# Weights loaded from their fourth byte on and rebuilt by a shift and a half-precision copy, keys transposed in the MLP's PSUM ring, another order of the steps

## The chip, the cores and the metric

The kernel runs on one core of one Trainium2 chip. The metric is the device time of one execution in microseconds (us), as a median of several runs. The engines of the core are named as in the profile: PE (TensorE matmul), PEld (TensorE weight load, which overlaps PE), DVE (VectorE), ACT (ScalarE), POOL (GpSimd) and SP (SyncE, which issues the transfers).

## What is computed

A gated linear attention (a recurrence over 768 tokens for 4 batches of 8 heads of width 48) is followed by a two-layer MLP with an unusual activation. Cut to what matters:

```python
for t in range(S):                                     # S = 768
    state = alpha[:, :, t, :, None] * state + einsum('bhd,bhe->bhde', k[:, :, t], v[:, :, t])
    y[:, :, t] = einsum('bhd,bhde->bhe', q[:, :, t], state)
x = y.transpose(0, 2, 1, 3).reshape(3072, 384)
h = x @ w_in                                           # 384 x 2048, float64 in memory
sp = maximum(h, 0) + log1p(exp(-abs(h)))
out = (h * erf(sp)) @ w_out                            # 2048 x 384, float64 in memory
```

The two weight matrices arrive as float64, everything else as float32.

## The kernel before

**Attention.** The tokens are cut into 24 chunks (`Chunk`, number n). A chunk loads alpha, k, q and v (`la lk lq lv`), makes decay products with two scans on DVE (`sb`, `sa`), scales k and q (`kk`, `qq`), and then on PE transposes the keys (`pn`, copied out by `kn` on ACT or `kd` on DVE), multiplies the state into the output (`qt`), makes scores (`ps`, masked on DVE by `mk`), multiplies scores by values (`sv`) and makes the state's update (`pu`, added on DVE by `ta` to the state that `td` has decayed). `pn`, `ps` and `pu` all write one PSUM tile, `both`. The output is copied to SBUF in two parts that together hold float32: `xh` on ACT (x_hi) and `xl` on DVE (x_lo, the remainder). `xp` and `xe` are another way to x_lo: PE subtracts x_hi in PSUM, ACT copies the rest out.

**MLP.** Two chunks make one of 12 blocks (`Moe`, 256 tokens). In a block each of 8 halves of the hidden units takes `hm` on PE (18 matmuls of 128x256 into a PSUM ring `h` of two buffers), `he` on ACT or `hd` on DVE (copy to SBUF), then by pairs of halves the activation: `u n1 n2 n3 g` on ACT, which switch between two function tables, and `ma mb z1 z2` on DVE. After that comes `ga` on ACT or `gd` on DVE (high part), `gl` on DVE (low part), and `om` on PE (12 matmuls of 128x384, added up in the two PSUM tiles `acc0` and `acc1`). `oe` on ACT or `ob` on DVE copies the sums out, `od` stores them. There is one pair of accumulators, so the first `om` of a block waits for the copies of the block before.

**Weights.** 12 tiles of w_in (512 columns) and 16 of w_out (384 columns) are made once (`Weight`, steps `w..i_n` and `w..o_n`). `wl` loads float64 as pairs of 32-bit words. ACT makes a float32 from the high word (`wy`) and the three bits of the low word (`wc`, or `wv` on DVE); DVE joins them (`wa`, `wb`); ACT rounds to the matmul's type (`wh`, or `wk` on DVE). The remainder is made on DVE (`wq`) or by two matmuls on PE into the ring `h` (`wp`) and a copy (`we`). The first `hm` of a group of hidden units needs its three tiles of w_in complete.

**Order.** All of it is one list of step names, `ORDER`, written out by hand or by a planner. Each engine runs its instructions in the order of the list (class `Queue`), so an instruction that waits holds everything behind it on its engine. `dw_n` are n matmuls on the identity that write nothing used.

Of the kernel before, what the change touches and what calls it, by code (L numbers as in the profile page):

```python
# [16 lines left out]
I16 = mybir.dt.int16  # L17
# [38 lines left out]
hm_2_0_1 who_13 wqo_13 z2_0_3 wco_14 ma_1_0 pn_6 he_2_0_1 wyo_14 wlo_15 wco_15 wyo_15 wao_14 om_0_2_1 kn_6 sv_6
ga_0_3_0 gl_0_3_0 pu_6 wao_15 ga_0_3_1 gl_0_3_1 xh_6 wbo_14 lv_7 om_0_3_0 u_1_1 lk_7 wbo_15 g_1_0 mb_1_0
hm_2_2_0 ic_6 la_7 who_15 wqo_15 who_14 wqo_14 om_0_3_1 u_1_2 n1_1_2 oe_0_1 od_0_1 oe_0_0 hm_2_2_1 z1_1_0 z2_1_0
ga_1_0_0 sb_7 lq_7 rc_7 gl_1_0_0 gd_1_0_1 n1_1_1 lq_8 xl_6 sa_7 gl_1_0_1 om_1_0_0 n2_1_2 n2_1_1 om_1_0_1
he_2_2_0 qq_7 kk_7 hm_2_3_0 n3_1_1 td_7 ma_1_1 mb_1_1 n3_1_2 he_2_2_1 ps_7 mk_7 qt_7 hm_2_3_1 g_1_1 u_1_3 z1_1_1  # L60
z2_1_1 u_2_1 ic_7 ga_1_1_0 sv_7 xh_7 ta_6 la_8 ga_1_1_1 lv_8 ma_1_2 pn_7 gl_1_1_0 om_1_1_0 gl_1_1_1 om_1_1_1
sb_8 he_2_3_0 mb_1_2 g_1_2 n1_1_3 he_2_3_1 n2_1_3 n3_1_3 lk_8 xl_7 hm_3_0_0 hm_3_0_1 z1_1_2 z2_1_2 rc_8 gd_1_2_0
gl_1_2_0 om_1_2_0 ma_1_3 he_3_0_0 ga_1_2_1 gl_1_2_1 om_1_2_1 g_1_3 he_3_0_1 td_8 hm_3_1_0 hm_3_1_1 mb_1_3 sa_8
u_2_0 n1_2_0 lk_9 n2_2_0 z1_1_3 z2_1_3 gd_1_3_1 kk_8 ga_1_3_0 la_9 gl_1_3_0 om_1_3_0 n3_2_0 lq_9 qq_8 kn_7
n1_2_1 n2_2_1 n3_2_1 he_3_1_0 od_0_0 he_3_1_1 gl_1_3_1 pu_7 ps_8 ma_2_0 qt_8 mb_2_0 om_1_3_1 sb_9 ma_2_1 mb_2_1
g_2_1 z1_2_1 ob_1_0 od_1_0 u_2_2 oe_1_1 hm_3_2_0 mk_8 z2_2_1 hm_3_2_1 g_2_0 ic_8 rc_9 gd_2_1_1 u_2_3 n1_2_2 sv_8
gd_2_1_0 gl_2_1_1 gl_2_1_0 xh_8 n2_2_2 ta_7 om_2_1_0 pn_8 z1_2_0 he_3_2_0 ic_9 sa_9 om_2_1_1 he_3_2_1 z2_2_0
gd_2_0_1 gl_2_0_1 n3_2_2 n1_2_3 kk_9 xl_8 lv_9 ma_2_2 hm_3_3_0 hm_3_3_1 ga_2_0_0 n2_2_3 n3_2_3 kn_8 qq_9 g_2_2
om_2_0_1 mb_2_2 td_9 qt_9 pu_8 ps_9 ma_2_3 gl_2_0_0 om_2_0_0 u_3_1 u_3_0 z1_2_2 he_3_3_1 mk_9 sv_9 g_2_3
he_3_3_0 lq_10 n1_3_0 z2_2_2 gd_2_2_0 gl_2_2_0 om_2_2_0 od_1_1 la_10 mb_2_3 gd_2_2_1 xh_9 sb_10 xl_9 hm_4_0_0  # L70
rc_10 n1_3_1 n2_3_1 n2_3_0 gl_2_2_1 n3_3_0 n3_3_1 sa_10 he_4_0_0 ta_8 ma_3_0 hm_4_0_1 he_4_0_1 om_2_2_1 g_3_0
z1_2_3 z2_2_3 ga_2_3_0 mb_3_0 u_3_2 ga_2_3_1 z1_3_0 hm_4_2_0 hm_4_2_1 ma_3_1 lk_10 kk_10 u_3_3 qq_10 he_4_2_0
la_11 gl_2_3_0 g_3_1 n1_3_3 pn_9 kn_9 gl_2_3_1 n2_3_3 n3_3_3 om_2_3_0 td_10 om_2_3_1 oe_2_1 oe_2_0 qt_10 lk_11
z2_3_0 mb_3_1 z1_3_1 hd_4_2_1 z2_3_1 gd_3_1_0 sb_11 gl_3_1_0 ga_3_0_1 pu_9 ps_10 mk_10 ta_9 gl_3_0_1 n1_3_2
n2_3_2 n3_3_2 ic_10 rc_11 ic_11 hm_4_1_0 he_4_1_0 lv_11 hm_4_1_1 td_11 he_4_1_1 om_3_1_0 ma_3_2 pn_10 ga_3_0_0
gl_3_0_0 u_4_0 om_3_0_1 od_2_1 g_3_2 sa_11 u_4_1 mb_3_2 z1_3_2 ga_3_1_1 ma_3_3 g_3_3 lq_12 gl_3_1_1 z2_3_2
hm_4_3_0 hm_4_3_1 om_3_1_1 om_3_0_0 u_4_2 n1_4_2 ga_3_2_1 kd_10 lv_10 pu_10 n1_4_1 n2_4_1 kk_11 la_12 mb_3_3
lq_11 qq_11 ps_11 sv_10 xh_10 sb_12 he_4_3_1 gl_3_2_1 om_3_2_1 gd_3_2_0 gl_3_2_0 mk_11 ta_10 rc_12 xl_10 z1_3_3
z2_3_3 gd_3_3_1 od_2_0 pn_11 n1_4_0 n2_4_0 om_3_2_0 kn_11 gl_3_3_1 n3_4_0 ga_3_3_0 gl_3_3_0 qt_11 ma_4_0 pu_11
# [12 lines left out]
lq_15 sb_15 om_5_1_1 rc_15 gl_5_2_0 ma_5_3 u_6_2 pn_14 u_6_1 td_15 om_5_2_0 gd_5_0_0 kn_14 sv_14 sa_15 qq_15
# [51 lines left out]
def gla_moe(ctx: ExitStack, tc: tile.TileContext, q, k, v, alpha, w_in, w_out, out):  # L144
    nc = tc.nc


    M, CPB, P, NP, NI, TC = q.shape
    B, H, S = M * NI, 2 * NP, CPB * TC
    W = NP * NI * TC  # L150
    NT, DM = out.shape
    FF = w_in.shape[1]
    TB = 256
    NBLK = NT // TB
    KT = DM // P
    NF = FF // P
    GT = 4
    NG = NF // GT
# [485 lines left out]
    class Weight:  # L644
# [23 lines left out]
        def wx(self):  # L668
            self.wy(on_dve)
# [277 lines left out]
```

## Time and profile before

| | us |
|---|---|
| median of 3 runs (lowest, highest) | 516.27 (515.26, 516.82) |
| span of the profiled execution, first to last instruction | 513.9 |
| PE busy in the span | 504.0 (98%) |
| PEld busy | 481.7 (94%) |
| DVE busy | 488.2 (95%) |
| ACT busy | 465.8 (91%), of it 64 table loads: 82.1 |

The profiled execution has no time beside its span; the median of the runs is 2.35 us above that span, which is taken for what lies around it. "Busy" is the share of the span in which an engine had an instruction running. Matmuls are pipelined, so a busy PE is not a PE at its peak; the time that PE needs is read from the distance between the starts of groups of matmuls. An instruction that starts before the one ahead of it has ended overlaps it: sums of durations are larger than busy time.

### The profile page before, as it was taken

The page shows a single profiled execution, that of the slowest core. Times are in us where ns is not written, and L with a number is a line of the kernel's source. Part 1 is how long each engine was busy: PE and PEld are TensorE (multiplying, and loading weights), DVE is VectorE, ACT ScalarE, POOL GpSimd, SP SyncE. Part 2 cuts the span into 40 slices and gives each one's busy share as a digit, 9 for nine tenths or more (in the row PEclk, how much of TensorE's full clock was granted, in tenths as well). Part 3 has the DMA queues.
Part 4 walks back from the last instruction along what each step waited for, and adds up shares of the span by engine and source line. Part 5 has one row for each costly group of instructions (what it writes and reads, how often), then busy time and mean ns, then how long its engine had stood idle before and what let it go on. Part 6 is the DMA issues. An engine that isn't in the chain of part 4 may idle for free.

```text
span 513.9 us, 16869 instructions
## 1 busy us (share of the span) xinstructions
PE 504.0 (98%) x7465; PEld 481.7 (94%) x7465; DVE 488.2 (95%) x655; ACT 465.8 (91%) x637; POOL 6.5 (1%) x41
## 2 busy tenths in 40 slices
PE   6999999999999999999999999999999999999996
PEld 6689999999999999999999999999999999999996
DVE  6999999999999999999999999999998999999894
ACT  6999999999999989999898888899988899898992
POOL 3000000000000000000000000000000000000000
PEclk9999999999999999999999999999999999999999
DMA  8954363321121032122023211301231310000000
GB/s 324 401 200 176 117 188 131 97 81 60 58 74 44 22 99 78 45 73 83 23 78 107 80 41 60 85 15 44 68 111 54 90 58 32 3 1 32 0 32 34
DMA packets 21387, 43.69 MB, mean 85 GB/s; under 512 B 2368, under 2 KB 5440, under 8 KB 21312
## 3 DMA queue, kind: packets, MB, share of 16 engines
q1 hardware_dynamic: 21312, 42.59, 25.4%
q8 instruction: 59, 0.97, 0.8%
q14 instruction: 16, 0.13, 0.1%
HBM read 37.86 MB, written 4.72 MB: 83 GB/s over the span
## 4 chain that ended last, share of the span: by engine, by line
PE 64%; DVE 18%; ACT 12%; issue 4%; DMA 1%; POOL 1%; DVEq 0%; POOLq 0%; ACTq 0%
PE acc L211 29%; PE h__112 L211 13%; PE h__111 L211 12%; PE both L211 4%; PE py L211 4%; DVE t L211 2%; DVE gl__104 L211 1%; ACT L211 1%; DVE gl__103 L211 1%; DVE w__98 L211 1%; DVE w__100 L211 1%; PE warm L211 1%; ACT w__97 L211 1%; DMA s__87<-in_moe_w_out_dram 1%; DVE w__97 L211 1%
## 5 line engine op out<-in xcount | busy, mean ns | idle before, releaser
L211 ACT ACT_TABLE_LOAD x64 | 82.1, 1283 | 1.9 <-PEq L901 0.9
L211 PE MATMUL acc<-wo_hi,gh__102 128*128 128x384 f32 x192 | 44.7, 346 | 0.1
L211 PE MATMUL acc<-wo_hi,gh__101 128*128 128x384 f32 x192 | 43.9, 348 | 0.1
L211 PE MATMUL acc<-wo_lo,gh__102 128*128 128x384 f32 x192 | 43.0, 337 | 0.2 <-DVE wo_lo L211 0.2
L211 PE MATMUL acc<-wo_hi,gl__104 128*128 128x384 f32 x192 | 43.1, 337 | 0.0
L211 PE MATMUL acc<-wo_lo,gh__101 128*128 128x384 f32 x192 | 41.6, 336 | 0.0
L211 PE MATMUL acc<-wo_hi,gl__103 128*128 128x384 f32 x192 | 41.6, 337 | 0.0
L211 PEld LDWEIGHTS acc<-wo_lo,gh__102 128*128 128x128 f32 x192 | 34.2, 188 | 0.5 <-DVE wo_lo L211 0.5
L211 PEld LDWEIGHTS acc<-wo_hi,gl__104 128*128 128x128 f32 x192 | 34.3, 188 | 0.0
L211 PEld LDWEIGHTS acc<-wo_hi,gl__103 128*128 128x128 f32 x192 | 34.0, 188 | 0.2 <-DVE gl__103 L211 0.2
L211 PEld LDWEIGHTS acc<-wo_lo,gh__101 128*128 128x128 f32 x192 | 34.1, 188 | 0.0
L211 PEld LDWEIGHTS acc<-wo_hi,gh__101 128*128 128x128 f32 x192 | 31.6, 188 | 1.9 <-DVE gh__101 L211 0.4
L211 PEld LDWEIGHTS acc<-wo_hi,gh__102 128*128 128x128 f32 x192 | 32.6, 188 | 0.8 <-DVE gh__102 L211 0.2
L211 DVE TENSOR_TENSOR_SCAN B<-raw_a,back 128x520 f32<-128x520 f32 x24 | 29.6, 1233 | 4.0 <-POOL T L266 3.9
L211 DVE TENSOR_TENSOR_SCAN A<-raw_a,start 128x520 f32<-128x520 f32 x24 | 29.6, 1233 | 0.2
L211 ACT ACTIVATE s__88<-s__88 128x1024 f32<-128x1024 f32 x22 | 23.2, 1056 | 1.0 <-DVE t L211 0.9
L211 ACT ACTIVATE s__86<-s__86 128x1024 f32<-128x1024 f32 x20 | 21.2, 1058 | 1.9 <-DVE t L211 1.8
L211 PE MATMUL h__112<-x_hi__107,wi_hi 128*128 128x256 f32 x144 | 21.7, 286 | 0.3 <-ACT wi_lo L211 0.3
L211 PE MATMUL h__111<-x_hi__107,wi_hi 128*128 128x256 f32 x144 | 21.4, 284 | 0.0
L211 PE MATMUL h__111<-x_hi__108,wi_hi 128*128 128x256 f32 x144 | 21.1, 282 | 0.0
L211 PE MATMUL h__112<-x_hi__108,wi_hi 128*128 128x256 f32 x144 | 21.1, 282 | 0.0
L211 PE MATMUL h__112<-x_lo__109,wi_hi 128*128 128x256 f32 x144 | 21.0, 281 | 0.0
(338 smaller groups left out, 1420.5 us busy)
## 6 DMA issues: line engine op xcount, KB each, us to landing
raw_a<-in_alpha_dram SPq DMA_DIRECT2D x24, 260.5 KB, 2.8
raw_k<-in_k_dram SPq DMA_DIRECT2D x24, 256.0 KB, 3.1
raw_q<-in_q_dram SPq DMA_DIRECT2D x24, 256.0 KB, 3.3
raw_v__113<-in_v_dram SPq DMA_DIRECT2D x12, 256.0 KB, 3.3
raw_v__114<-in_v_dram SPq DMA_DIRECT2D x12, 256.0 KB, 3.6
out_dram<-o__106 SPq DMA_DIRECT2D x12, 192.0 KB, 2.0
out_dram<-o__105 SPq DMA_DIRECT2D x12, 192.0 KB, 2.6
s__85<-in_moe_w_out_dram SPq DMA_DIRECT2D x4, 384.0 KB, 3.7
```

What stands on the lines that cost most here:

```text
L211: ins = made(*args, **kw)
```

## The change

- A weight tile is loaded from the fourth byte on, as bytes (the arrays are padded by one column for it). The first 32-bit word of a pair then holds the low 27 bits of the float32 to be made (after a shift by 5), the second its sign and high exponent in its low byte.
- `wy`, `wc`, `wv`, `wb` go. `wr` on DVE shifts the second word up into a tile of its own, `wd` on ACT copies that, as half precision, into the upper half of its own words, and `wa` on DVE shifts the first word and joins.
- Of the 28 remainders, 6 of w_in (9 before) and 3 of w_out (none before) are made on PE; three chunks use `xp` and `xe` in place of `xl`.
- `pn` writes a buffer of the MLP's PSUM ring `h` in place of `both`; the state has one tile in place of two; the ring of high parts has 4 buffers in place of 2; the hs tile is taken at `he` and no longer at `hm`.
- `dw` grows from 25 matmuls to 41, of which 30 stand first; the matmuls that clear `both` come behind the first 30.
- `ORDER` is another list. New steps that it does not use are left out below.

```diff
-    gp = Ring(gpool, gh=([P, 2, TB], F32R, 2), gl=([P, 2, TB], F32R, 2), ...
+    gp = Ring(gpool, gh=([P, 2, TB], F32R, 4), gl=([P, 2, TB], F32R, 2), ...
...
-    Ts = [[at.tile([P, NI * NP * HD], F32, name="T", tag=f"T{m}{n}", bufs=1) for n in range(2)] for m in range(M)]
+    Ts = [at.tile([P, NI * NP * HD], F32, name="T", tag=f"T{m}", bufs=1) for m in range(M)]
...
         def pn(self):
-            self.pn_ = both
+            self.pn_ = ps_h.tile([P, 512], F32, name="pn", tag="h")
...
         def hm(self, g, half):
-            if half == 0:
-                self.hs[g] = self.pl.h.tile([P, GT * TB], F32, name="hs", tag="hs")
...
         def he(self, g, half, copy=on_act):
+            if self.hs[g] is None:
+                self.hs[g] = self.pl.h.tile([P, GT * TB], F32, name="hs", tag="hs")
...
     class Weight:
+            if self.wide:
+                self.src = src.bitcast(U8)[:, 8 * c * n + 3 : 8 * (c + 1) * n + 3]
...
         def wl(self):
             if self.wide:
-                self.st = self.pool.tile([P, self.n, 2], I32, name="wst", tag=self.tag)
-                sp.dma_start(out=self.st.rearrange("p n two -> p (n two)"), in_=self.src.bitcast(I32))
+                st = self.pool.tile([P, self.n, 2], I32, name="wst", tag=self.tag)
+                flat = st.rearrange("p n two -> p (n two)").bitcast(U8)
+                sp.dma_start(out=flat, in_=self.src)
+                self.low, self.rest = st[:, :, 0], st[:, :, 1]
...
-        def wy(self, copy=on_act):
-            if self.wide:
-                copy(self.parts()[0], self.st[:, :, 1].bitcast(F32), 2.0**-112)
...
-        def wc(self):
-                act.activation(self.parts()[1], low[:, :, 3], AF.Copy, scale=1 / 32, bias=-31 / 64)
...
+        def wr(self):
+            if self.wide:
+                buf = keep_w.tile([P, 2, 512], F32, name="wbuf", tag="w")
+                self.top, self.z = buf[:, 0, : self.n], buf[:, 1, : self.n]
+                dve.tensor_scalar(
+                    out=self.top.bitcast(I32), in0=self.rest, scalar1=24, scalar2=None, op0=ALU.logical_shift_left
+                )
...
         def wd(self):
             if self.wide:
+                high = self.top.bitcast(F16).rearrange("p (n two) -> p n two", two=2)[:, :, 1]
+                act.activation(high, self.top, AF.Copy)
...
         def wa(self):
             if self.wide:
-                y, z = self.parts()
                 dve.scalar_tensor_tensor(
-                    out=z, in0=y.bitcast(I32), scalar=3, in1=z, op0=ALU.logical_shift_left, op1=ALU.bitwise_or
+                    out=self.z.bitcast(I32), in0=self.low, scalar=5, in1=self.top.bitcast(I32),
+                    op0=ALU.logical_shift_right, op1=ALU.bitwise_or,
                 )
...
-        def wb(self):
...
         def dw(self, n):
             for _ in range(n):
                 pe.matmul(out=self.t[:, :P], lhsT=ident, rhs=ident, start=True, stop=True)
+            for bank in range(2 * clear):
+                pe.matmul(
+                    out=both[:, bank, NP * TC : NP * (TC + D)], lhsT=ident, rhs=Ts[0][:, : NP * D],
+                    start=True, stop=True,
+                )
```

The start of DVE's instructions. In the rows w__97 to w__100 are the buffers in which weights are put together, hs__90 and up and s__85 and up are loaded weights, B and A the scans' results, sT the masked scores. Before:

```order
L211 SCALAR_TENSOR_TENSOR B<-raw_a,back 128x520
L211 RECIPROCAL start<-B 128x8
L211 SCALAR_TENSOR_TENSOR A<-raw_a,start 128x520
L211 SCALAR_TENSOR_TENSOR w__97<-w__97 128x512 x2
L211 SCALAR_TENSOR_TENSOR w__98<-w__98 128x512 x2
L211 TENSOR_TENSOR raw_k_118<-raw_k_118,B 128x512
L211 SCALAR_TENSOR_TENSOR w__99<-w__99 128x512 x2
```

The same place after the change:

```order
L203 TENSOR_SCALAR w__97<-hs__90 128x512
L203 SCALAR_TENSOR_TENSOR B<-raw_a,back 128x520
L203 RECIPROCAL start<-B 128x8
L203 SCALAR_TENSOR_TENSOR A<-raw_a,start 128x520
L203 TENSOR_SCALAR w__98<-s__85 128x384
L203 TENSOR_SCALAR w__99<-hs__91 128x512
L203 SCALAR_TENSOR_TENSOR w__97<-hs__90,w__97 128x512
L203 TENSOR_TENSOR raw_k_120<-raw_k_120,B 128x512
```

DVE now begins with a weight's shift and reads two tiles of w_in and one of w_out before the keys are scaled.

PE's instructions around the first `hm` (the row with x_hi and wi_hi) before, with `wp` (w__97 and wi_hi,minus), `pn` (ident,raw_k) and `wp` ahead of it:

```order
L211 MATMUL h__112<-w__97,ident 128x512
L211 MATMUL h__112<-wi_hi,minus 128x512
L211 MATMUL both<-ident,raw_k_119 128x128 x4
L211 MATMUL h__111<-w__100,ident 128x512
L211 MATMUL h__111<-wi_hi,minus 128x512
L211 MATMUL h__112<-x_hi__107,wi_hi 128x256 x6
```

The same place after the change:

```order
L203 MATMUL both<-raw_v__116,kn 48x48 x16
L203 MATMUL both<-raw_q_118,raw_k_120 64x64 x16
L203 MATMUL py<-raw_q_118,T 32x64 x32
L203 MATMUL h__113<-ident,raw_k_120 128x128 x4
L203 MATMUL h__114<-w__99,ident 128x512
L203 MATMUL h__114<-wi_hi,minus 128x512
L203 MATMUL h__113<-x_hi__109,wi_hi 128x256 x6
```

Chunk 2's `ps`, `qt` and `pn` and chunk 1's `pu` have moved ahead of the first `hm`; `pn` now writes `h`; the last `wp` ahead of the first `hm` is that of w_in tile 9, of the last group.

PE's instructions where block 10 ends and block 11 begins, after the change (the row with `good` is a one-column matmul of a range check):

```order
L203 MATMUL acc<-wo_hi,gh__104 128x384 x2
L203 MATMUL acc<-wo_lo,gh__104 128x384 x2
L203 MATMUL acc<-wo_hi,gl__106 128x384 x2
L203 MATMUL both<-ones,good 1x1
L203 MATMUL acc<-wo_hi,gh__101 128x384 x4
```

The last `om` of block 10 and the first of block 11 now stand side by side; before, two `hm` stood between them.

## Rows read from the trace of the kernel before

**Rows 1.** Windows: us, then busy us (instructions) of PE, PEld, DVE, ACT, POOL; PEclk, DMA share, GB/s
```profile
0.00:28.88 28.88, 23.87 (x312) 17.00 (x312) 24.39 (x39) 24.48 (x50) 4.38 (x19) 1.00 0.96 366
28.88:108.88 80.00, 79.73 (x1487) 76.07 (x1488) 79.65 (x126) 79.71 (x136) 0.49 (x5) 1.00 0.40 131
108.88:509.84 400.96, 400.41 (x5669) 388.59 (x5668) 384.21 (x492) 361.13 (x452) 1.67 (x17) 1.00 0.18 56
509.84:513.90 4.06, 0.00 (x1) 0.00 (x0) 0.00 (x0) 0.49 (x1) 0.00 (x0) 1.00 0.28 101
```

**Rows 2.** Chain that ended last: start us, us, what
```profile
9.94 1.10 PE h__111 L211 x3
...
173.50 2.08 PE acc L211 x12
175.59 2.13 PE h__112 L211 x18
...
184.64 0.79 PE py L211 x53
185.43 0.98 PE both L211 x64
186.41 2.32 PE h__112 L211 x18
```

**Rows 3.** Timeline of PE at its first MLP matmul: start us, us, what, idle before
```profile
28.88 0.99 PE L211 MATMUL h__112<-x_hi__107,wi_hi 128*128 128x256 f32 x6 [0.26 <-ACT wi_lo L211]
```

**Rows 4.** Groups by form: mean ns of the operations that weights are made of
```profile
L211 DVE SCALAR_TENSOR_TENSOR w__100<-w__100 128x384 int32<-128x384 int32 x10 | 5.5, 549 | 0.0
L211 DVE SCALAR_TENSOR_TENSOR w__97<-w__97 128x512 int32<-128x512 int32 x6 | 4.1, 681 | 0.0
L211 DVE TENSOR_SCALAR w__98<-s__85 128x384 int32<-128x384 int32 x2 | 0.7, 350 | 0.0
L211 DVE CAST gh__101<-hs__90 128x512 fp32r<-128x512 f32 x4 | 1.7, 420 | 0.1
L211 ACT ACTIVATE w__98<-hs__95 128x512 f32<-128x512 f32 x1 | 0.7, 691 | 0.0
L211 ACT ACTIVATE w__97<-s__87 128x384 f32<-128x384 f32 x2 | 1.1, 573 | 0.0
L211 ACT ACT_TABLE_LOAD x64 | 82.1, 1283 | 1.9 <-PEq L901 0.9
```

**Rows 5.** Timeline of the first microseconds: start us, us, what, idle before
```profile
0.91 0.38 SPq L211 DMA_DIRECT2D raw_a<-in_alpha_dram  x1
1.34 0.42 SPq L211 DMA_DIRECT2D hs__90<-in_moe_w_in_dram  x1
1.52 0.29 POOL masks.py:199 TENSOR_SCALAR_AFFINE_SELECT ident<-ident 128x128 f32<-128x128 f32 x1
...
3.92 1.24 DVE L211 TENSOR_TENSOR_SCAN B<-raw_a,back 128x520 f32<-128x520 f32 x1 [3.92 <-POOL T L266]
5.04 1.22 ACT L211 ACTIVATE w__97<-hs__90 128x512 f32<-128x512 f32 x2 [2.56 <-DMA hs__90<-in_moe_w_in_dram]
```

**Rows 6.** Windows of the first `dw` alone: us, busy us of PE (matmul passes), PEclk, DMA share, GB/s
```profile
4.72:8.77 4.05, 4.05 (x19) 1.00 1.03 396
8.77:9.78 1.01, 1.01 (x10) 1.00 1.01 378
```

**Rows 7.** DMA issues: KB each, median us to landing
```profile
raw_a<-in_alpha_dram SPq DMA_DIRECT2D x24, 260.5 KB, 2.8
raw_k<-in_k_dram SPq DMA_DIRECT2D x24, 256.0 KB, 3.1
```

**Rows 8.** Groups: copies out of the PSUM ring, and an activation on the same engine
```profile
L211 ACT ACTIVATE hs__90<-h__111 128x512 f32<-128x512 f32 x9 | 5.3, 585 | 0.0
L211 ACT ACTIVATE s__88<-s__88 128x1024 f32<-128x1024 f32 x22 | 23.2, 1056 | 1.0 <-DVE t L211 0.9
```

**Rows 9.** Timeline: the copy of the first accumulator at the end
```profile
508.84 0.49 ACT L211 ACTIVATE o__105<-acc 128x384 f32<-128x384 f32 x1 [3.27 <-PE acc L211]
```

More of the change, by code (lines that the diff above doesn't have):

```diff
@@ L151, in gla_moe @@
     NT, DM = out.shape
-    FF = w_in.shape[1]
+    FF = w_in.shape[1] - 1
     TB = 256
@@ L218, in __getattr__ @@
             return call
[L220 to L221 removed]
+    queues = [Queue(e) for e in (nc.tensor, nc.vector, nc.scalar, nc.sync, nc.gpsimd)]
+    pe, dve, act, sp, pool = queues
     ra = raw.tile([P, 1 + L], F32, name="raw_a")
@@ L262, in need @@
             act.preload_act_table_set(name)
-    Ts = [[at.tile([P, NI * NP * HD], F32, name="T", tag=f"T{m}{n}", bufs=1) for n in range(2)] for m in range(M)]
-    for t in Ts[0] + Ts[1]:
+    Ts = [at.tile([P, NI * NP * HD], F32, name="T", tag=f"T{m}", bufs=1) for m in range(M)]
+    for t in Ts:
         nc.gpsimd.memset(t, 0.0)
-    Tv = [[t.rearrange("p (i a d) -> p i a d", i=NI, a=NP)[:, :, :, :D] for t in pair] for pair in Ts]
+    Tv = [t.rearrange("p (i a d) -> p i a d", i=NI, a=NP)[:, :, :, :D] for t in Ts]
     both = ps_at.tile([P, 2, 512], F32, name="both", tag="b")
-    pe.matmul(
-        out=both[:, 1, NP * TC : NP * (TC + D)], lhsT=ident, rhs=Ts[0][0][:, : NP * D],
-        start=True, stop=True,
-    )
     def on_act(out, in_, scale=1.0):
@@ L450, in ta @@
             if self.first:
-                act.activation(Tv[self.m][0], U, AF.Copy)
+                act.activation(Tv[self.m], U, AF.Copy)
             else:
-                dve.tensor_tensor(out=Tv[self.m][0], in0=Tv[self.m][1], in1=U, op=ALU.add)
+                dve.tensor_tensor(out=Tv[self.m], in0=Tv[self.m], in1=U, op=ALU.add)
         def xh(self):
@@ L594, in z2, with to_hi, gh, ga @@
             )
-        def ga(self, g, half):
+        def to_hi(self, g, half, copy):
             gg = self.hs[g][:, half * 512 : (half + 1) * 512]
             gh = self.pl.gp.tile([P, 2, TB], F32R, name="gh", tag="gh")
-            act.activation(gh.rearrange("p a t -> p (a t)"), gg, AF.Copy)
+            copy(gh.rearrange("p a t -> p (a t)"), gg)
             self.gg[g, half] = gg, gh
+        def gh(self, g, half):
+            self.to_hi(g, half, lambda out, in_: pool.dma_start(out=out, in_=in_))
+        def ga(self, g, half):
+            self.to_hi(g, half, on_act)
         def gd(self, g, half):
-            gg = self.hs[g][:, half * 512 : (half + 1) * 512]
-            gh = self.pl.gp.tile([P, 2, TB], F32R, name="gh", tag="gh")
-            dve.tensor_copy(out=gh.rearrange("p a t -> p (a t)"), in_=gg)
-            self.gg[g, half] = gg, gh
+            self.to_hi(g, half, on_dve)
         def gl(self, g, half):
@@ L675, in wv @@
                 )
-        def wc(self):
-            if self.wide:
-                low = self.st.rearrange("p n two -> p (n two)").bitcast(U8).rearrange("p (n b) -> p n b", b=8)
-                act.activation(self.parts()[1], low[:, :, 3], AF.Copy, scale=1 / 32, bias=-31 / 64)
-        def halves(self, kind, k):
-            return self.parts()[1].bitcast(kind).rearrange("p (n two) -> p n two", two=2)[:, :, k]
         def wd(self):
             if self.wide:
-                act.activation(self.halves(F16, 1), self.st[:, :, 1].bitcast(F32), AF.Copy, scale=2.0**-60)
@@ L712, in wk, with wm @@
             self.wh(on_dve)
+        def wm(self):
+            pool.dma_start(out=self.hi, in_=self.z)
         def wq(self):
@@ L931 @@
                 a = wide
-        elif name == "moe_w_in":
-            a = a[order]
+        else:
+            a = _np.pad(a[order] if name == "moe_w_in" else a, ((0, 0), (0, 1)))
         a = _np.ascontiguousarray(a)
```

256 lines of the change are left out of this document (116 added, 140 removed).

## The prediction, made blind

> **What bounds the kernel now.** I read the windows first, cut at two starts: PE's first MLP matmul, and the end of its last. In [rows 1] the reader is to see three stretches. Until 28.88 us, where the first `hm` starts [rows 3], PE is busy 23.87 us, but much of that is `dw` and waiting; DVE is busy 24.39 us of the 24.96 from its first instruction at 3.92 [rows 5], and ACT 24.48. From 28.88 to 108.88 PE, DVE and ACT are all busy over 79.6 of 80 us. From 108.88 to 509.84 PE stays at 400.41 of 400.96, while DVE has 16.75 us to spare and ACT 39.8. So the time is: the front until 28.88, then 480.96 us of PE without a gap, then a tail of 4.06.
>
> Whether PE is itself the bound in the middle, or is held by DVE, the chain of waits tells: an `om` of 12 matmuls takes 2.08 us and an `hm` of 18 takes 2.13, and only one behind small matmuls takes 2.32 [rows 2]. Such rows repeat over all 96 `hm` and 96 `om`. If I give each group of matmuls behind 28.88 the median of groups of its kind with the same kinds before and behind, the 480.96 become 478.3: 2.7 us is what PE lost there to others. A change that only frees ACT or DVE cannot win more than that behind the front.
>
> **Part by part, the engines' load.** For 12 tiles of 512 and 16 of 384 columns: DVE loses `wb`, 12 x 0.681 + 16 x 0.549 = 17.0 us, and three `wv`, 1.1; it gains `wr`, a single-source shift from the same 8-byte step as `wv`: 16 x 0.350, and for 512 columns the 0.420 of a single-source copy, 5.0 [rows 4]; 10.6 together. Other steps that went to DVE (4 `kd`, 4 `hd`, 3 `wq` of w_in, and one each of `gd`, `ob`, `wk`, less 3 `wq` of w_out and 3 `xl`) add about 5. Net -2.5 of 488. ACT loses `wy` and 25 `wc` of 28, about 32.8 us at 0.69 and 0.56 to 0.57 each, and gains 28 `wd`. No row has a write of half precision with a step; the nearest are `wy`'s own 0.691 and 0.573 [rows 4], which I take: 17 us. Twice that is the upper bound; below those rows nothing on ACT speaks for a gain. But the new order switches tables 74 times for 64, 10 x 1.283 = 12.8 us [rows 4]. With 5 us of steps that went to DVE, ACT is at -8 of 466. Neither is the bound behind 108.88, so the place where this can count is the front.
>
> **The front.** Until the first `hm` DVE had 38 instructions and part of one more, which by durations are 27.1 us and took 24.39, a factor of 0.90 (instructions overlap) [rows 1]. In the new order the first `hm` needs `wq` of tile 0, and up to it stand 44: 9 + 3 `wr`, 8 + 3 `wa`, 3 each of `sb`, `rc`, `sa`, `kk`, `qq`, `mk`, 2 `wq`, 1 `td`, by durations 27.9, at 0.90 25.1 us. The load is no smaller, because three tiles of w_out and all of chunk 2's preparation now come ahead. DVE also starts later: its first instruction is now a shift of a loaded tile. That tile's load came at 5.04 when issued at 1.34 [rows 5]; issued at 0.91, 4.6. With the 0.6 us that DVE lost in this stretch before, it is through at 4.6 + 25.1 + 0.6 = 30.3. PE's last `wp` ahead of it waits for `wa` and `wh` of tile 9, some 1.7 us earlier on DVE, and takes 1.10 [rows 2], which leads to the same place. **First `hm`: 30.4**, bounds 29.2 (DVE without a pause) and 32 (below).
>
> ACT has 23.6 us of durations ahead of that point instead of 29.2, so it waits for DVE and no longer shares the bound. That is why freeing it gives nothing here. The `dw` of 30: PE starts it when POOL has made the identity, 1.85 us, and not at 3.92. Its passes take 213 ns (19 in 4.05 us, the level of 1.2 GHz) until 8.77 and then 112 ns (2.4 GHz) [rows 6], though the granted column reads 1.00 in both. If the rise comes as long after PE's first instruction as before, 4.85 us, 60 passes end at 10.8 and the four that clear `both` at 11.5. `ps` of chunk 0 waits behind them; its inputs are ready at 10.2 and DVE wants the result for `mk` at 11.95, gets it at 12.2. That 0.3 is inside the 0.6. If the rise stays at 8.77, it is 1 us more: part of the upper bound.
>
> **What PE has left.** Ahead of the first `hm` PE has now also done `ps`, `qt`, `pn` of chunk 2 and `pu` of chunk 1: 0.98 for `ps` and `pu`, 0.79 for `qt` [rows 2], and four passes of 0.112 [rows 6] for `pn`, 2.2 us. Behind it stand 480.96 - 2.2 = 478.7. Of the three `xp` one is behind it: two matmuls of 192 columns, under the 0.12 us each that 256 columns take in [rows 2] (2.13 / 18), so 0.2. Switches between large and small groups fall by a tenth in number, but fewer pass through `pn`, the only small group that costs an `hm` nothing before it: the same median count gives +0.3, bounds -1 and +1. At block 10 to 11 the accumulators must be copied with no `hm` between: DVE's copy of `acc1` (0.55 for 384 columns, as in [rows 4]) ends 0.2 to 0.5 behind the point at which PE is ready; I take 0.3. Reuse of the ring `h`, with `pn` in it: +0.3 (rival below). The state in one tile makes `ta` wait for `qt`, but `qt` stands ahead of `ta` everywhere. Together 30.4 + 478.7 + 0.2 + 0.3 + 0.3 + 0.3 = 510.2.
>
> **The tail.** Before, the copy of `acc0` ran while PE still worked on `acc1`, from 508.84 on [rows 9], and only one copy was left [rows 1]. Now ACT's list has the copy of `acc1` first, so that of `acc0`, complete a microsecond earlier, stands behind it, and its store last: +0.4. Span 510.2 + 4.06 + 0.4 = **514.7**, 0.8 above 513.9; with the median's 2.35 around it 517.0. I keep some of the 2.7 us for PE, since with 8 us less on ACT some waits will go: -0.4. **516.6.**
>
> **The loads.** Rows of 4096 and 3072 bytes now begin three bytes past a word. The transfers are near their limit in the front, 396 GB/s at a share of 1.03 [rows 6] and 0.96 over the whole of it [rows 1]. The nearest row is alpha: its rows of 2084 bytes begin at multiples of 4 that are no larger power of two, and land in 2.8 us against 3.1 for 2048 [rows 7]. I take nothing, with twice the time as the other bound.
>
> The Trainium skill speaks against the change here: "DMA: Bandwidth & Descriptors", section "How a descriptor splits into AXI transactions", says that reads start at 256-byte boundaries, so a start between them costs a transaction more. By that, an estimate, 17 in place of 16 for 4096 bytes would add 6% to each load, some 0.9 us over the 11 loads of the front if loads came last there, and the sum would be 517.5. The row of alpha shows no such cost, but its 2084 bytes were loaded alone.
>
> **Rivals.** (1) *Faster: DVE holds PE in the middle.* All three engines are full from 28.88 to 108.88. Up to the last weight step DVE's queue is 115.8 us by durations for 93.0 of PE's work, 114.5 for 88.6 before: 4.4 - 1.2 = 3.2 us in the change's favour, less 0.7 of later start. If that is what PE waits for, it gains 2.5 and most of the tail's and ring's loss is not noticed: 513.8. For it: DVE is never idle there. Against: the even 2.08 and 2.13. Chance 0.27.
> (2) *Slower: the ring `h`.* It has two buffers, and 22 `pn` are added to 105 uses. Places where PE comes back to a buffer with less than 2.2 us of its own work between: 8 before behind 25 us, all at 2.13; now 15, six of them under 2, the shortest 1.14 (block 5). A copy takes 0.585, and an activation of 1.056 ahead of it on ACT [rows 8] makes that 1.64. It decides if the copies come late by an activation in most of these places: 15 x 0.25 = 3.7 us, 520.4. Chance 0.19.
> (3) *Slower: loads from an odd byte take twice as long.* A load of 512 KB at 400 GB/s takes 1.3 us, 8 to 11 of them in the front, which has no room: 10 us or more, 527. Chance 0.08.
> (4) *The two-byte write of `wd` is slow.* At twice 17 us ACT is at +9 in all, and in the front at 29, as before; no change of the time, inside the forecast.
>
> **How the numbers follow.** Forecast 516.6 (a run of this kernel tells 0.3%, 1.55 us, from no change): chance 0.46, range 514.8 to 518.4 from the bounds of the first `hm` and of the switches. Faster by over 0.3%: rival 1, 0.27. Slower: rivals 2 and 3 and the forecast's upper end, 0.27. The range that leaves out 2 in 10 goes from 512.6 (rival 1 with 1.2 us of an early first `hm`) to 520.6.
>
> **What would show it.** The first `hm` at 30.4 (29.2 to 32), with DVE full and ACT idle some 5 us before it; `hm` and `om` at 2.13 and 2.08 behind it; the wait of `om` at block 11 under 0.5; the last two copies one behind the other. Wrong: an idle PE in front of `hm` with a copy of `h` as releaser (2), DVE waiting for transfers before 28 us (3), or PE's stretch behind the first `hm` shorter than 477 (1).

## The result and the profile after

The changed kernel takes 520.09 us in the median of 15 runs (516.85 to 523.23), the kernel before, run beside it, 515.82 (515.26 to 516.82): a ratio of 1.0078, 95% interval 1.0059 to 1.0098. It is 0.8% slower, and its runs scatter over 6.4 us where those of before scatter over 1.6. The profiled execution took 518.62 us, its span is 516.8.

The windows of the changed kernel, cut as in [rows 1] at the first `hm` and at the end of PE's last matmul (same columns):

```profile
0.00:34.22 34.22, 29.74 (x481) 23.60 (x482) 25.55 (x46) 22.38 (x46) 3.73 (x18) 1.00 0.96 353
34.22:114.22 80.00, 80.00 (x1498) 76.95 (x1497) 79.18 (x128) 79.11 (x124) 0.59 (x5) 1.00 0.44 135
114.22:511.50 397.28, 397.25 (x5529) 386.36 (x5527) 376.42 (x488) 360.00 (x444) 1.91 (x16) 1.00 0.17 51
511.50:516.80 5.30, 0.00 (x0) 0.00 (x0) 0.00 (x0) 0.87 (x2) 0.00 (x0) 0.92 0.22 77
```

Beside [rows 1]: the front is 5.34 us longer (34.22 for 28.88), PE's stretch behind it 3.68 shorter (477.28 for 480.96), the tail 1.24 longer (5.30 for 4.06). Together 2.9 us, the difference of the spans. In the longer front DVE is busy 1.2 us more and ACT 2.1 less than before; the rest of the added time those two stand idle. PE is busy 5.9 us more there, with the longer `dw` and the groups that moved ahead of `hm`.

PE's timeline in the front (start us, us, what, idle before) has two holes whose releaser is "issue", which means that PE waited for nothing that the profile shows:

```profile
18.84 0.58 PE L203 MATMUL both<-raw_v__115,kn 64*48 64x48 f32 x32
19.23 0.35 PE L203 MATMUL both<-raw_q,raw_k 48*64 48x64 f32 x9
20.58 0.57 PE L203 MATMUL both<-raw_q,raw_k 48*64 48x64 f32 x23 [0.99 <-issue]
...
29.57 0.66 PE L203 MATMUL both<-raw_q,raw_k 48*64 48x64 f32 x32
30.16 0.86 PE L203 MATMUL py<-raw_q,T 48*32 48x64 f32 x64
32.64 0.66 PE L203 MATMUL h__113<-ident,raw_k 128*128 128x128 f32 x4 [1.61 <-issue]
33.13 1.02 PE L203 MATMUL h__114<-w__99,ident 128*128 128x512 f32 x2
33.59 0.80 PE L203 MATMUL h__114<-wi_hi,minus 128*128 128x512 f32 x1
34.22 0.87 PE L203 MATMUL h__113<-x_hi__109,wi_hi 128*128 128x256 f32 x6
```

The first hole is inside one group: 9 of `ps`'s 32 matmuls run, then nothing for a microsecond, then 23. No buffer and no operand changes between the 9th and the 10th. If PE's instructions are counted from its start (weight loads, matmuls, and its sequencer's few, 7 and 13 by then), the holes stand behind the 449th and behind the 961st, 512 apart. The transfers of the stretches just ahead of the two holes (18.0 to 19.4 us, and 30.0 to 31.2) contain one packet each of another kind; columns are packets, MB, share of 16 engines:

```profile
q8 instruction: 1, 0.02, 4.6%
...
q8 instruction: 1, 0.02, 5.6%
```

By the trace's list of packets these have 16,384 bytes, which for 256 instructions is 64 bytes each, and end at 19.18 and 31.17 us. PE goes on 1.40 and 1.47 us later. The queue is PE's: it carries 60 such packets in the execution, room for 15,360 instructions, and the windows above count some 15,000 weight loads and matmuls. So the reading is that PE had run out of program. `pu` of chunk 1 with `ps` and `qt` of chunk 2 (64, 64 and 128 instructions, and two of the sequencer among them) fill the 256 up to the 961st, and PE ran through them in 1.6 us (29.18 to 30.81).

DVE's timeline in the front shows what else was late:

```profile
4.68 0.43 DVE L203 TENSOR_SCALAR w__97<-hs__90 128x512 int32<-128x512 int32 x1 [4.68 <-DMA hs__90<-in_moe_w_in_dram]
...
8.86 0.36 DVE L203 TENSOR_SCALAR w__98<-s__85 128x384 int32<-128x384 int32 x1 [0.69 <-DMA s__85<-in_moe_w_out_dram]
...
21.21 0.69 DVE L203 TENSOR_TENSOR sT<-both,mask 128x512 f32<-128x512 f32 x1 [0.81 <-PE both L203]
...
31.24 0.69 DVE L203 TENSOR_TENSOR wi_lo<-w__98,wi_hi 128x512 fp32r<-128x512 f32 x1
```

The 0.81 us at 21.21 is `mk` waiting for the `ps` that the first hole cut in two. DVE's last step for the first `hm` ends at 31.93, so DVE was not what `hm` waited for. Behind the second hole PE itself still had `pn` and `wp` to do, 1.58 us up to 34.22. Without that hole's 1.61 us `hm` would have started at 32.6, without both holes at 31.6.

At the end both copies and both stores come one behind the other (ACT and SP):

```profile
511.53 0.49 ACT L203 ACTIVATE o__108<-acc 128x384 f32<-128x384 f32 x1 [7.94 <-PE acc L203]
511.92 0.48 ACT L203 ACTIVATE o__107<-acc 128x384 f32<-128x384 f32 x1
...
512.05 0.34 SPq L203 DMA_DIRECT2D out_dram<-o__108  x1
512.48 0.38 SPq L203 DMA_DIRECT2D out_dram<-o__107  x1
```

From the last store's issue to the end of the span it is 4.3 us; before, where the two stores were issued 1.04 us apart, 3.5.

### The profile page after: what moved, and what is told of

It reads as the page before. It is cut to its first block, busy times and chain, and to the rows that moved or that the text cites. A ratio compares the mean times of both kernels' runs of the same rounds, so it can differ in the third digit from the quotient of the medians.

```text
span 516.8 us, 16909 instructions
## 1 busy us (share of the span) xinstructions
PE 507.0 (98%) x7505; PEld 486.9 (94%) x7505; DVE 481.2 (93%) x660; ACT 462.4 (89%) x614; POOL 6.2 (1%) x39
## 4 chain that ended last, share of the span: by engine, by line
PE 98%; issue 1%; ACT 0%; POOL 0%; POOLq 0%
PE acc L203 39%; PE h__113 L203 23%; PE h__114 L203 22%; PE py L203 7%; PE both L203 5%; PE warm L203 2%; ACT o__108 L203 0%; ACT o__107 L203 0%; POOL ident masks.py:199 0%; POOL inv L235 0%; POOL mask L221 0%; POOL ident masks.py:197 0%; POOL sums L233 0%; POOLq L919 0%; POOL ones L230 0%
## 5 line engine op out<-in xcount | busy, mean ns | idle before, releaser
L203 PE MATMUL acc<-wo_hi,gl__106 128*128 128x384 f32 x192 | 43.1, 337 | 0.0
L203 PE MATMUL acc<-wo_hi,gl__105 128*128 128x384 f32 x192 | 41.5, 337 | 0.0
L203 PEld LDWEIGHTS acc<-wo_hi,gl__106 128*128 128x128 f32 x192 | 34.2, 188 | 0.0
L203 PEld LDWEIGHTS acc<-wo_hi,gl__105 128*128 128x128 f32 x192 | 34.0, 188 | 0.1
L203 PE MATMUL h__113<-x_hi__109,wi_hi 128*128 128x256 f32 x162 | 24.4, 286 | 0.0
L203 PE MATMUL h__113<-x_hi__109,wi_lo 128*128 128x256 f32 x162 | 23.6, 281 | 0.0
L203 PE MATMUL h__113<-x_lo__111,wi_hi 128*128 128x256 f32 x162 | 23.5, 280 | 0.0
L203 PE MATMUL acc<-wo_hi,gh__104 128*128 128x384 f32 x96 | 22.7, 339 | 0.0
L203 PE MATMUL acc<-wo_lo,gh__104 128*128 128x384 f32 x96 | 22.4, 337 | 0.0
L203 PE MATMUL h__114<-x_hi__110,wi_hi 128*128 128x256 f32 x150 | 22.4, 285 | 0.0
L203 PEld LDWEIGHTS h__113<-x_hi__109,wi_hi 128*128 128x128 f32 x162 | 21.7, 188 | 0.7 <-ACT kn L203 0.2
L203 PE MATMUL h__114<-x_hi__110,wi_lo 128*128 128x256 f32 x150 | 21.8, 281 | 0.0
L203 PE MATMUL h__114<-x_lo__112,wi_hi 128*128 128x256 f32 x150 | 21.8, 281 | 0.0
L203 ACT ACTIVATE s__88<-s__88 128x1024 f32<-128x1024 f32 x20 | 21.0, 1052 | 0.7 <-DVE t L203 0.7
L203 ACT ACTIVATE s__86<-s__86 128x1024 f32<-128x1024 f32 x20 | 21.1, 1057 | 0.5 <-DVE t L203 0.4
L203 ACT ACTIVATE s__87<-s__87 128x1024 f32<-128x1024 f32 x20 | 21.2, 1058 | 0.1
L203 PE MATMUL acc<-wo_hi,gh__101 128*128 128x384 f32 x96 | 21.1, 340 | 0.0
L203 PE MATMUL acc<-wo_hi,gh__102 128*128 128x384 f32 x96 | 21.1, 341 | 0.0
L203 PEld LDWEIGHTS h__113<-x_lo__111,wi_hi 128*128 128x128 f32 x162 | 21.1, 188 | 0.0
```

The source lines that it names most:

```text
L203: ins = made(*args, **kw)
```

## The experiments

Theory A: PE's program comes in packets of 256 instructions, and PE stalls where it runs through one packet faster than the next one arrives. Rivals: B, the loads from an odd byte are late; C, the second hole is a wait of `qt` itself or of what stands around it; D, there are simply too many instructions ahead of the first `hm`. All runs are timed beside the kernel before on the same chip. There were several chips, on which the kernel before took 515.82 to 516.46 us in the median, so rows are best compared by their ratios.

| kernel | PE's holes up to 38 us (behind which PE instruction) | first `hm` | median (lowest to highest) | ratio to before |
|---|---|---|---|---|
| changed | 0.99 (449), 1.61 (961) | 34.22 | 520.09 (516.85 to 523.23) | 1.0059 to 1.0098 |
| changed, again | 0.75 (449), 2.16 (961) | 35.16 | 519.18 (518.85 to 522.83) | 1.0059 to 1.0113 |
| old end | 0.76 (449), 2.16 (961) | 34.44 | 517.81 (516.53 to 523.68) | 1.0012 to 1.0057 |
| `qt_2` behind the first `hm` | 1.39 (1217) | 30.91 | 517.71 (517.02 to 519.16) | 1.0016 to 1.0037 |
| first `dw` in fewer instructions | 0.86 (961) | 31.47 | 516.80 (516.30 to 517.29) | 0.9991 to 1.0010 |
| more small instructions | 0.57 (1217) | 31.57 | 516.92 (516.40 to 518.36) | 1.0010 to 1.0031 |
| loads from byte 0 | 0.65 (449), 2.94 (961) | 36.16 | 520.75 (517.02 to 523.39) | 1.0036 to 1.0099 |
| first `dw` in fewer, old end | no row of a hole | 31.60 | 515.41 (514.60 to 517.32) | 0.9976 to 0.9996 |

**The place of the packets' ends.** Three edits move it. The first takes one group away from it:

```diff
-... ps_2 whi_9 qt_2 mk_2 pn_2 ... wpi_9 hm_0_0_1 wdo_9 ...
+... ps_2 whi_9 mk_2 pn_2 ... wpi_9 hm_0_0_1 qt_2 wdo_9 ...
```

> The changed kernel with qt_2 (64 small matmuls) moved behind the first hm. Theory A (PE runs out of instructions: its program arrives in packets of 256 instructions, which come late while the transfers are full, and pu_1, ps_2 and qt_2 use up 256 in 2 us): the hole of PE at 31.0 to 32.6 us goes, no new one opens behind qt_2, the first hm starts at 32.0 to 32.4 in place of 34.2, the hole at 19.6 stays; time -2 us. Theory B (loads from an odd byte are late): the first hm stays at 34. Theory C (the hole belongs to qt_2 itself, its buffer or POOL's relay): it moves with qt_2 and opens behind it, after the first hm; time within 0.5 us of the changed kernel.

PE's timeline:

```profile
30.91 0.95 PE L203 MATMUL h__113<-x_hi__109,wi_hi 128*128 128x256 f32 x6
...
33.20 0.86 PE L203 MATMUL py<-raw_q,T 48*32 48x64 f32 x64
33.99 0.58 PE L203 MATMUL both<-raw_v__115,kn 64*48 64x48 f32 x32
...
35.28 0.98 PE L203 MATMUL h__114<-x_hi__109,wi_hi 128*128 128x256 f32 x6
37.65 0.87 PE L203 MATMUL h__114<-x_hi__109,wi_lo 128*128 128x256 f32 x6 [1.39 <-issue]
```

The hole behind the 961st instruction is gone, and `qt`, now at 33.20, has none behind it: C falls. The first `hm` is 3.3 us earlier, more than expected, because the first hole is missing too; there the packet came at 16.68 to 17.71 us instead of 18.15 to 19.18. The edit stands behind that place, so that part is luck. A new hole stands where nobody looked for one, in the middle of an `hm`, behind the 1217th instruction: 256 after the 961st. The time is 2.4 us below the changed kernel's.

The second edit leaves the order alone and makes the first `dw` of fewer, longer matmuls:

```diff
-            for _ in range(n):
-                pe.matmul(out=self.t[:, :P], lhsT=ident, rhs=ident, start=True, stop=True)
+            for _ in range(n // 4 if clear else n):
+                if clear:
+                    pe.matmul(
+                        out=self.t.rearrange("p (a b) -> p a b", a=4), lhsT=ident,
+                        rhs=ident.unsqueeze(1).broadcast_to([P, 4, P]), start=True, stop=True,
+                    )
...
-... lk_0 lq_0 dw_30 wlo_3 ...
+... lk_0 lq_0 dw_32 wlo_3 ...
```

> The changed kernel with the first dw as 8 matmuls of 512 columns in place of 30 of 128: PE is as long busy, in 88 fewer instructions. Theory A (PE runs out of instructions at every 256th): the places at which the packets end move by 88 instructions, the holes at 19.6 and 31.0 both go or shrink to under 0.5 us, first hm at 31.3 to 32.3; time -2 to -3 us, and the runs scatter less. Theories B (odd byte) and C (qt_2's own wait): holes and first hm stay, time as that of the changed kernel within 0.5 us.

```profile
19.42 0.66 PE L203 MATMUL both<-raw_q,raw_k 48*64 48x64 f32 x32
...
29.10 0.86 PE L203 MATMUL py<-raw_q,T 48*32 48x64 f32 x64
29.89 0.66 PE L203 MATMUL h__113<-ident,raw_k 128*128 128x128 f32 x4
...
31.47 0.87 PE L203 MATMUL h__113<-x_hi__109,wi_hi 128*128 128x256 f32 x6
...
35.01 0.39 PE L203 MATMUL both<-raw_v__115,kn 64*48 64x48 f32 x14 [0.86 <-issue]
```

`ps` at 19.42 runs in one piece, `pn` follows `qt` at once, and the 961st instruction now falls inside a `pu` behind the first `hm`, where a shorter hole is left (0.86 us, more than the 0.5 expected). The runs lie within 1.0 us instead of 6.4, and the time is 3.3 us lower, for an edit that takes no work from PE.

This run also shows what releases the first `hm` once the holes are gone. PE works from `pu` of chunk 1 at 28.11 to `hm` without a pause, and DVE's last step for `hm` is done 0.6 us before it, at 30.87:

```profile
30.18 0.69 DVE L203 TENSOR_TENSOR wi_lo<-w__98,wi_hi 128x512 fp32r<-128x512 f32 x1
```

So with this order PE's own steps ahead of `hm` decide, no longer DVE.

The third edit asks the opposite question, with 160 instructions more:

```diff
-... lk_0 lq_0 dw_30 wlo_3 ...
+... lk_0 lq_0 dw_12 wlo_3 ...
...
             for _ in range(n):
                 pe.matmul(out=self.t[:, :P], lhsT=ident, rhs=ident, start=True, stop=True)
+            for _ in range(58 * clear):
+                pe.matmul(out=self.t[:32, :32], lhsT=ident[:, :32], rhs=ident[:, :32], start=True, stop=True)
```

> The changed kernel with 18 of the first 30 dw passes replaced by 58 passes of 32 columns, about as long on PE: 160 instructions more ahead of everything else. Theory A (a packet of 256 instructions is asked for as PE comes to the packet before it, so what counts is how fast PE runs through each 256, not how many instructions there are): the borders move so that pu_1, ps_2 and qt_2 no longer fill one packet; no hole over 0.6 us before the first hm, first hm at 31 to 32.5, runs within 2 us of each other, time 516 to 517.5. Rival D (too many instructions ahead of the first hm, the sum counts): with 160 more the holes grow by 1 us or more, first hm at 35 or later, time 521 or more.

```profile
29.20 0.86 PE L203 MATMUL py<-raw_q,T 48*32 48x64 f32 x64
29.99 0.66 PE L203 MATMUL h__113<-ident,raw_k 128*128 128x128 f32 x4
...
31.57 0.87 PE L203 MATMUL h__113<-x_hi__109,wi_hi 128*128 128x256 f32 x6
...
34.83 0.33 PE L203 MATMUL both<-raw_v__115,kn 64*48 64x48 f32 x9 [0.57 <-issue]
```

More instructions, 3.2 us less time: D falls, and A holds in both directions. What counts is how the small groups lie against the packets' ends.

**The loads.** Every weight from byte 0 of an unpadded row:

```diff
-                self.src = src.bitcast(U8)[:, 8 * c * n + 3 : 8 * (c + 1) * n + 3]
+                self.src = src.bitcast(U8)[:, 8 * c * n : 8 * (c + 1) * n]
...
-            a = _np.pad(a[order] if name == "moe_w_in" else a, ((0, 0), (0, 1)))
+            a = a[order] if name == "moe_w_in" else a
```

> The changed kernel with all weights loaded from byte 0 of unpadded rows, so every row begins at a multiple of 3072 bytes; the weights that it makes are other numbers, of the same work (wr shifts right in place of left). Theory A: the holes stay, first hm at 34 within 0.7 us, the time stays within 1 us; 4096 byte packets take 159 ns in the median as before. Theory B (loads from an odd byte are what makes the front late): the first transfers land up to 1 us earlier, DVE's waits for transfers go, first hm at 32 or earlier, time -2 us or more.

The time is that of the changed kernel, and both holes are there; B falls. The first `hm` came at 36.16, later than theory A had it too, since the second hole was 2.94 us long. The first tiles landed 0 to 0.4 us earlier (3.5 us after issue for 3.8, 7.5 for 7.9, 5.9 for 5.9). Against this scatter such an effect on the time can only be bounded, not measured. This execution also shows why the runs scatter. Its windows around the second hole (columns as above, PEclk third from the end):

```profile
26.00:30.26 4.26, 4.26 (x138) 3.05 (x136) 3.85 (x7) 3.90 (x9) 0.00 (x0) 1.00 1.02 396
30.26:33.41 3.15, 0.21 (x23) 0.05 (x4) 1.72 (x5) 0.49 (x1) 0.28 (x1) 1.00 1.03 397
33.41:34.00 0.59, 0.58 (x4) 0.59 (x5) 0.00 (x0) 0.00 (x0) 0.00 (x0) 0.81 0.98 391
34.00:36.00 2.00, 2.00 (x5) 0.97 (x4) 0.49 (x1) 1.67 (x4) 0.00 (x0) 0.50 0.55 170
36.00:38.00 2.00, 2.00 (x13) 1.91 (x13) 2.00 (x4) 2.00 (x5) 0.00 (x0) 0.70 0.80 244
```

PE was idle 2.94 us, and behind that the granted clock is 0.81, 0.50 (the level of 1.2 GHz) and 0.70. A longer hole thus costs twice: once itself, and once in the steps behind it (2.74 us from the hole's end to `hm`, for 1.58 in the changed kernel). Of the changed kernel's 15 runs the 7 with a mean clock of 0.998 or more took 516.85 to 519.95 us, the 8 with 0.996 or less 520.09 to 523.23.

> The changed kernel once more, unchanged. Theory A: both holes again at the 449th and 961st PE instruction, the second 1.6 to 3.2 us long, and runs from 517 to 523; where the granted clock of the profiled run is under 0.998, it is down behind the second hole. Rival (the scatter has nothing to do with the holes): other places.

Run again, it has the same two holes at the same counts, the second 2.16 us long. The profiled execution kept its clock (1.00 behind the hole), so only the kernel with loads from byte 0 shows the fall of the clock in a trace; that the changed kernel's longer runs are such cases is inferred from their mean clock.

**The end.**

```diff
-... om_11_3_0 oe_11_1 oe_11_0 od_11_1 od_11_0
+... om_11_3_0 oe_11_0 od_11_0 oe_11_1 od_11_1
```

> The changed kernel with the list's end as before: oe_11_0 od_11_0 oe_11_1 od_11_1. Theory (two copies and two stores one behind the other at the end): the tail behind PE's last matmul goes from 5.3 to about 4.1 us and the time falls by 1.2 us, nothing else moves. Rival (the last store's landing varies by itself, only ACT's order counts): the tail falls by 0.4, the time by 0.4.

```profile
510.82 0.49 ACT L203 ACTIVATE o__107<-acc 128x384 f32<-128x384 f32 x1 [6.90 <-PE acc L203]
511.86 0.49 ACT L203 ACTIVATE o__108<-acc 128x384 f32<-128x384 f32 x1 [0.55 <-PE acc L203]
```

One copy is again hidden behind PE, whose last matmul ends at 511.83; the span is 515.9, so the tail is 4.07 us for 5.30. The medians differ by 2.3, more than the trace's 1.2, because the holes' scatter is in both. Without the long holes the comparison is cleaner:

> The first dw as 8 matmuls of 512 columns and the end of the list as before (the two separate edits together). Theory: the tail of 5.3 falls to 4.1 us, the rest as with the wide dw alone (first hm at 31.5, 516.8 us): 515.6 us, scatter of 1 us. Rival (the tail's 1.2 us is landing that varies): 516.4.

515.41 us against 516.80 is 1.4 us, but on two chips; by the ratios to before, 1.0001 and 0.9986, it is 0.8 us. The trace's 1.2 lies between. The two edits together take all of the loss back: the ratio to before is 0.9986 (0.9976 to 0.9996). This version is faster than both kernels, by 0.14% over the one before.

**Attempts to gain more from the packets**, all three with these two edits. First the other `dw` made wide as well, then `qt_2` moved too (as above), and apart from these a second `hm` taken forward:

```diff
-... ta_0 dw_7 wai_6 ... wri_0 dw_3 whi_6 ...
+... ta_0 dw_8 wai_6 ... wri_0 dw_4 whi_6 ...
```

```diff
-... hm_0_0_1 wdo_9 ta_1 wao_9 pu_2 wlo_2 wdi_8 whi_5 wei_9 lk_4 ... wri_10 hm_0_0_0 xh_2 ...
+... hm_0_0_1 wdo_9 ta_1 wei_9 wao_9 hm_0_0_0 pu_2 wlo_2 wdi_8 whi_5 lk_4 ... wri_10 xh_2 ...
```

> As the one with the wide first dw and the old end, and the dw of 7 and 3 passes as 2 and 1 of 512 columns: 28 instructions fewer again. Theory A: the border that with the wide first dw fell behind the third hm (hole of 0.6 us at 34) falls later, in a stretch of large matmuls: the hole goes, 515.1 us. Rival: the packet comes later by as much, and the hole stays: 515.6.

> The three edits together: wide dw, old end, qt_2 behind the first hm. Theory A: first hm at 30.8 to 31.2, qt_2's 0.8 us follow behind it, and small groups stand between hm's so that no 256 instructions pass in under 5 us; 514.8 to 515.3 us. Rival: behind the first hm qt_2, sv_2 and pu_2 stand close (2.4 us for 256 instructions in the run with qt_2 moved alone, hole of 1.7 us at 36), and the hole comes back: 516.5.

> The wide first dw and the old end, with hm_0_0_0 taken forward to stand behind hm_0_0_1 and ahead of pu_2 (and wei_9, whose buffer it takes, ahead of wao_9). Theory A: the hole at the 961st PE instruction, in pu_2 at 33.8 to 34.7, goes, since the packet is there before PE comes to it; 0.5 us less than 515.4: 514.9. Rival (hm_0_0_0 waits for wei_9's copy by as much, or later steps come late): 515.4 or more.

All missed their forecast; their ratios to before are 0.9999, 0.9992 and 1.0005. With the other `dw` wide as well: 516.04 us, a hole of 0.61 us behind the 961st instruction, since the packet came no earlier (32.6 us, with the first `dw` alone 32.5). With `qt_2` behind `hm` too: 516.09, 0.73 us at the same count. With `hm_0_0_0` moved forward: no hole behind the 961st, as expected, but 516.16; the attention steps behind it are late, and PE waits for a copy instead:

```profile
37.52 0.47 PE L203 MATMUL py<-x_hi__110,minus 128*128 128x192 f32 x2 [0.67 <-ACT x_hi__110 L203]
```

A hole of under a microsecond behind the first `hm` was not worth an edit of the order.

**Does DVE hold PE behind the first `hm`?** Once with more on DVE, in `wa` of the version with both edits, and once with less, in the order of the kernel before:

```diff
+                if self.twice:
+                    dve.scalar_tensor_tensor(
+                        out=self.z.bitcast(I32), in0=self.low, scalar=5, in1=self.top.bitcast(I32),
+                        op0=ALU.logical_shift_right, op1=ALU.bitwise_or,
+                    )
```

> The wide first dw and the old end, with the joining of a weight tile on DVE done twice (the same result) for the 17 tiles that come behind the first hm: 4 x 0.69 + 13 x 0.55 = 9.9 us more on DVE in the 80 us behind it, where DVE was 78.9 us busy. If DVE holds PE there (the prediction's first rival): PE's stretch from the first hm to its last matmul is longer by 4 us or more, 519 us or more. If PE is its own bound there and DVE's work is only early: longer by under 1 us, 515.4 to 516.4.

```diff
-... td_2 lq_2 wyi_11 wbo_12
+... td_2 lq_2 wyi_11
...
-he_0_0_0 la_3 sb_3 wbi_11 wbo_0 wci_10 ...
+he_0_0_0 la_3 sb_3 wci_10 ...
```

> The kernel before, without the 18 wb that come behind the first hm (3 x 0.681 + 15 x 0.549 = 10.3 us off DVE between 28.9 and about 105 us; these weight tiles then lack their sign, the work behind them is the same). If DVE holds PE there, as the prediction's first rival says: PE's stretch behind the first hm gets shorter, up to the 2.7 us that PE loses to others, the time falls by 1.5 to 2.7 us. If PE is its own bound there, as the forecast says: under 0.5 us.

The 80 us behind the first `hm`, with more on DVE:

```profile
31.58:111.58 80.00, 73.97 (x1316) 70.05 (x1315) 79.05 (x131) 72.16 (x115) 0.47 (x4) 0.98 0.43 141
```

and with less, in the kernel before:

```profile
29.25:109.25 80.00, 79.80 (x1489) 76.47 (x1490) 72.60 (x109) 79.77 (x136) 0.50 (x5) 1.00 0.40 130
```

9.9 us more cost 9.1 of PE's stretch (486.97 us for 477.83; 524.17 us in all). That is the outcome that was expected if DVE holds PE. It shows that DVE has under 1 us of slack there, not that it is the bound. 10.3 us less leave DVE idle for 7.4 of the 80 and gain nothing: PE's stretch is 480.77 us for 480.96, the ratio 0.9993 (0.9984 to 1.0001). So in the kernel before PE is the bound there. In the changed kernel PE has no idle time either (80.00 of 80 us), but less work on DVE was not tried in it.

## Why the prediction was right or wrong

- **What bounds the kernel**: right. PE has not one row of idle time between 35 and 511 us after, and taking 10 us off DVE in the kernel before gains nothing. The front, the stretch and the tail were the right three terms.
- **First `hm` at 30.4 (bounds 29.2 to 32)**: wrong by 3.8 us; this is the step that failed. DVE's work was right (25.1 us forecast, 24.9 measured up to 31.93), its start too (4.6, measured 4.68). But the step took DVE for what releases `hm` and said that PE's last `wp` "leads to the same place". What the runs show is PE's own path, which is later. 2.6 of the 3.8 us are the two holes in PE's program, 0.99 and 1.61, which the sum left out altogether: with the holes moved away and the same order of steps `hm` starts at 31.47 to 31.60, inside the bounds. Of the 1.2 us that are left, by the run with the first `dw` in fewer instructions, 0.6 are DVE's waits, put too small (it ends at 30.87, not 30.3; the wait for a w_out tile alone is 0.93 there), and 0.6 are PE's steps, which end behind DVE. With `qt_2` moved behind it `hm` starts at 30.91. The prediction priced every instruction that was moved ahead of `hm` by its time on PE (2.2 us for `ps`, `qt`, `pn`, `pu`) and none by its place in PE's program, although it moved 256 small ones to one spot and put 64 more in `dw` ahead.
- **`dw` of 30 and the clearing of `both`**: 0.5 us late (clears end at 12.05, forecast 11.5), because the passes took 213 ns for 5.5 us and not 4.85. Inside the allowance.
- **PE's stretch, 478.7 + 0.2 + 0.3 + 0.3 + 0.3 - 0.4 = 479.4**: 477.28, so 2.1 too long. The terms for the ring `h` and for block 10 to 11 were mis-sized: 0 each, since no `hm` or `om` waits. The term for switches had the wrong sign. Behind 100 us, from the starts of the groups, `om` takes 2.121 us in the mean for 2.163 before, `sv` 0.788 for 0.817, `ps` 0.565 for 0.602, while `hm` takes 2.186 for 2.150 and `pn` 0.425 for 0.365; together about 1.3 us less. Which moves of the order did that was not tried, so the cause of the shorter stretch stays open.
- **The tail, +0.4**: +1.24. The copies stood one behind the other, as said. Not counted was the time from the last store's issue to the end, 4.3 us for 3.5 (stores issued 0.43 us apart for 1.04).
- **The span, 514.7 - 0.4 = 514.3**: 516.8, by the +3.8, -2.1 and +0.8 above. The time around it was 1.8 us in this execution. The median lies another 1.5 above it. With the first `dw` in fewer instructions the scatter is 1.0 us for 6.4, so most of it hangs on the holes.
- **ACT**: not the bound, as said. `wd` is dearer than the `wy` row it was taken from, 0.79 and 0.64 us for 0.69 and 0.57 [rows 4], without consequence.
- **The loads from an odd byte**: taken as free, and free within what can be measured in the time. The estimate by the Trainium skill of 0.9 us over the front ("DMA: Bandwidth & Descriptors", section "How a descriptor splits into AXI transactions") is not borne out as time. In the landings, 0 to 0.4 us later out of 3.5 to 7.9, such a cost is neither shown nor excluded.
- **The rivals**: (1) fell as far as it was tried: DVE was full and yet did not hold PE in the kernel before. (2) fell: PE has no idle row that names a copy of the ring behind 35 us. (3) fell with the loads from byte 0. (4) was harmless as said. The result lies inside the wide range, 512.6 to 520.6, by luck: rivals 2 and 3, which its upper end allowed for, both fell, the kernel is slower for a cause that none of them names, and the errors of the front and of PE's stretch had opposite signs.

## What to carry to other kernels

Where an engine's idle row says "issue" and stands in the middle of a group, count the engine's instructions from its start: holes a multiple of 256 apart, each behind a packet of the kind "instruction", mean that the program came late. The word "issue" alone does not: in the run with more work on DVE a hole of 2.44 us with "issue" stands behind the 2701st instruction, between two borders, and the last packet had ended 7.5 us earlier. Before dense small matmuls are moved together, look how fast the engine would run through 256 of them, and keep long instructions between. Into how many instructions dummy work is cut moves the packets' ends with it: here 88 fewer and 160 more helped alike. And the last copies should leave in the order in which their sums are complete.

## What was not expected of the hardware

- PE goes on 1.3 to 1.5 us after the end of a late packet, in all eight holes behind the 449th and 961st instruction of the four executions that have both. The packet itself takes 1.0 to 1.1 us there. With 256 small matmul instructions in 1.6 us this makes a hole of 1.6 to 2.9 us. That full transfers make the packet late is not shown: behind 40 us, where the transfers are lighter, such packets of the changed kernel took 0.88 to 1.53 us.
- The Trainium skill ("Runtime: NRT & Kernel Launch", section "Instruction fetch mechanics") says that the program is refilled in blocks of 256 instructions through a DMA queue and that this is "mostly hidden". The trace agrees with the 256; hidden it is behind large matmuls, not here. When exactly a packet is asked for stays open: after PE came to the 450th instruction the next packet started 4.2 us later (24.81), after the 706th 0.9 us later (30.09).
- The kernel before has such a hole too: its `ps` of chunk 1 is cut behind the same 449th instruction, for 0.19 us, 1.36 us after the end of a packet at 20.23. It went unread in the prediction, as "issue" with a small number.

```profile
20.83 0.57 PE L211 MATMUL both<-raw_q,raw_k 48*64 48x64 f32 x23
21.59 0.35 PE L211 MATMUL both<-raw_q,raw_k 48*64 48x64 f32 x9 [0.19 <-issue]
```

- An idle time of 2.94 us of PE was followed by a granted clock of 0.50 for over 2 us.
